# An FNet layer with a ReGLU beside it: three moved steps, and the last 192 rows of h as a twelfth pair with short products

## The chip, the cores and the metric

One core of one Trainium2 chip runs the whole program. The metric is the device time of one execution in microseconds (us); "the time before" is the median of three runs. The matmuls run on TensorE (PE in the profile), elementwise work on VectorE (DVE), ScalarE (ACT) and GpSimd (POOL). SyncE (SP) computes nothing: it issues transfers. GpSimd issues transfers too. Each engine takes its instructions from its own queue, in order.

## The reference

All data are float32, S = 2048 tokens, D = 640 features, F = 1728 hidden features of the ReGLU. Cut to what is computed:

```python
xn = (x - mean(x)) / sqrt(var(x) + 1e-5)                 # layernorm over the 640 features
a = einsum("sd,ed->se", xn, dft_hid_re)
b = einsum("sd,ed->se", xn, dft_hid_im)
fnet = einsum("ts,se->te", dft_seq_re, a) - einsum("ts,se->te", dft_seq_im, b)
gate, up = xn @ W_gate, xn @ W_up                        # 640 x 1728 each
h = gate * (gate > 0) * up                               # 2048 x 1728
out = x + fnet + h @ W_down                              # W_down is 1728 x 640
```

The three weights of the ReGLU are drawn 64 times larger than the rest. The DFT matrices are inputs like any other.

## The kernel before

**Arithmetic.** Every product is made of three matmuls (`mm3`, L127 to L132): each float32 operand is cut into a high part in TensorE's reduced format and a low part (the remainder), and the matmuls are high·high, high·low and low·high, summed in one PSUM accumulator of 128 x 512 (a bank; there are eight). `split` (L123) makes the two parts: the high by a copy on ACT (L124), the low by a subtraction on DVE (L125). Products of 2 x 2 block matrices are done by a Winograd scheme: seven products of sums and differences of blocks in place of eight, so the operands need further sums and differences on DVE.

**Phase 1, up to about 350 us: layernorm and the DFT over the sequence.** The tokens are taken in eight groups of 256 (g from 0 to 7; NH = 4 is half of them), the columns of the DFT matrices in four chunks c of 512. The host reorders the 640 features into blocks; `K14` is the first 384 of a group's columns, `K2` the last 256 (called a21 for the first four groups). For the first groups nothing can be multiplied until the layernorm has made the group's high and low, so `first_stream` (L533) interleaves group by group: for chunk 0 the products of group n (`next_products`), for chunk 1 those of the same group (`product`), and, while these run, the layernorm of group n + 1 (`next_group`, L250). The work of the engines in `next_group` is pinned in program order. It is, per group of two token rows j: statistics (L204) on DVE; the high of the next DFT block on ACT (L257); a tiny GpSimd instruction that waits for the DVE low before it (`behind_vector`, L248, writes `root_t`), and two GpSimd subtractions for the low of that DFT block (L255); square root and mean on ACT; subtraction of the mean on DVE (`ln_center`, L225), the reciprocal, the high on ACT (`ln_high`, L231), the subtraction and the high for the second j; the refined inverse root (L218 to L221); the two lows on DVE (`ln_low`, L235). For g < NH there follows the scaling of the a21 columns on DVE (L276, two instructions) and their copy to their place in SBUF, a transfer issued by GpSimd (`keep_a21`, L238 to L240). For g >= NH all 640 columns are normalised at once. In `first_stream` the split of chunk 1's DFT block (L570) is issued after the layernorm's last DVE and ACT instruction (`late["ln"]`, `late["high"]`). When the last group of the first half is through chunk 0, `keep_first` (L593) copies the three accumulators of chunk 0 out on ACT (L121), since the second half uses the same banks anew.

**Phase 2, about 350 to 745 us: gate, up and h.** 26 blocks `gate_up(n)`, 13 of 128 hidden features for each half q of the tokens, plus `gate_up_rest` for the last 64 features. The blocks of h go to memory: `hd[q]` holds 13 blocks of 128 rows, `hrest[q]` the last 64. Beside the blocks DVE and ACT prepare what phase 3 needs of W_down and of the DFT over the hidden axis: `pair_weights(k, n)` (L966) loads pair k of two 128-row blocks of weights in block n - 1, makes four sums on DVE and a high and a low in block n, and stores them (1 MB) to `wparts` from GpSimd's queue in block n + 1. There are NPAIR = 11 pairs, five of the DFT and six of W_down, at blocks 13 to 23. At the very end `lead_load` and `lead_split` (L1003, L1009) prepare the first unit of phase 3.

**Phase 3, from 730 us to the end: `project(q)` for q = 1, then 0.** Out of the results of phase 1 (`pqd`) and h, out = x + fnet + h @ W_down is formed in transposed tiles of 128 features x 512 tokens: five feature blocks, two column chunks per half. The contraction consists of six units of one or two pairs each: three of the DFT over the hidden axis (pairs (0, 1), (2, 3), (4)) and three of h (pairs (0, 1), (2, 3), (4, 5)), that is rows 0 to 1535 of h. Seven Winograd products run over the units one after another: B11, T1, B21, T2, B22, T3, T4. A unit has three steps: `load` (transfers issued by SP), `prepare` (for T1, T2, T3, T4 a subtraction of two raw tiles on DVE, L1110; the split into the ring buffer; the split of the weights where they come raw) and `run` (the matmuls on two accumulators, on three for B11, T1, B21 and B22). `read` adds finished accumulators to tiles y on DVE (`add_y`, L1214), which `get_y` (L1206) has filled with x from memory (L1211); `get_y` stands behind each product's fourth unit.

Rows 1536 to 1663 of h (the thirteenth block) and the last 64 rows are not in a pair: `plain_block` and `plain_rest` prepare them beside product B21, and `plain_run` multiplies them plainly, with three matmuls per tile for the block and two for the 64 rows (high and low of these are stacked on the 128 partitions). In each half these are ten tiles of five matmuls: three tiles behind B21, three behind B22, and behind T3 the two tiles `("o", i)`, which hold the plain product alone, and the two accumulators ("a", i) that T4 then adds to.

**What sets the order.** `drive(far, ahead)` (L722) walks through the list `todo`: at position i it issues the prepare step of position i - 2, the load of position i, the reading of i - 5 and the matmuls of i - 4. In phase 3 the engines SP and GpSimd keep this written order (`manual_schedule`, L1266); a scheduler orders PE, DVE and ACT around the pins, where `in_turn` (L138) holds a split behind the third last low. In phase 2 PE, DVE and ACT are in written order. The tile pools of phase 3 (L1056) are rings: `ring2` has 3 buffers, `wts` 5, `wraw` 4, `raws` 24; a transfer into a buffer waits until its former content has been used, and a pool that lies over the memory of phase 2 waits for the last use there. The y tiles of before lie over a weight buffer of phase 2 (`gw1`), whose last use is the lead unit's.

Of the kernel before, what the change touches and what calls it, by code (L numbers as in the profile page):

```python
# [7 lines left out]
F32 = mybir.dt.float32  # L8
# [43 lines left out]
NPAIR = KD + NF // 2  # L52
# [6 lines left out]
def fnet_reglu_kernel(  # L59
# [190 lines left out]
    def next_group(g, b, raw, before):  # L250
# [18 lines left out]
        late["high"] = pin([ln_high(g, xs, mv, 1, cs)])[0].ins  # L269
# [4 lines left out]
        late["ln"] = pin(ln_low(g, xs, j, cs) for j in range(SG))[-1].ins  # L274
        if g < NH:
            late["ln"] = pin(nc.vector.tensor_scalar(xs[:, j, K2], xs[:, j, K2], mv[:, j, 0:1], stat[:, 1, g, j : j + 1],  # L276
                                                     op0=OP.subtract, op1=OP.mult) for j in range(SG))[-1].ins
# [255 lines left out]
    def first_stream(c, name, g):  # L533
# [25 lines left out]
        def prepare():  # L559
# [4 lines left out]
            if (n > 0 or c > 1) and "b" not in t:  # L564
# [401 lines left out]
    def pair_weights(k, n):  # L966
# [3 lines left out]
        def load():  # L970
            t["z"] = z = pool("prep").tile([P, Y12 + 2 * P], F32, name="pw")
            wa, wb = pair(k, 1)
            for w, o1, o2 in ((wa[0], Y11, Y21), (wb[0], Y12, LOW + Y22)):
                nc.sync.dma_start(z[:, o1 : o1 + 2 * P], w[:, : 2 * P])
                nc.sync.dma_start(z[:, o2 : o2 + 2 * P], w[:, 3 * P :])
# [16 lines left out]
    def pair(k0, n):  # L992
# [3 lines left out]
        f = 2 * (k0 - KD)  # L996
        w = wd[f * P : (f + 2 * n) * P].rearrange("(k i p) n -> k i p n", i=2, p=P)
# [58 lines left out]
    for n, b, side in (("wraw", 4, "left"), ("ring2", 3, "left"), ("wts", 5, "left"), ("raws", 24, "left"), ("plain", 1, "right"), ("y", 1, "right")):  # L1056
        open_pools[n] = ctx.enter_context(tc.tile_pool(name=n, bufs=b, side=side, reuse_waits="tile"))

    def project(q):
        c0, c1 = 2 * q, 2 * q + 1  # L1060
        units = [("hid", u) for u in HID_UNITS] + [("f", u) for u in F_UNITS]
        raws, B, y, plain = {}, {}, {}, {}

        def get(kind, u):
            what, ks = units[u]
            o = raws[kind, u] = pool("raws").tile([P, 2, CH], F32, name="rw")[:, : len(ks)]
            col, row = int(kind in ("B12", "B22")), int(kind in ("B21", "B22"))
            if what == "hid":
                nc.sync.dma_start(o, pqd[(c0, c1)[col]][row][:, ks[0] : ks[-1] + 1])
            else:  # L1070
                nc.sync.dma_start(o, hd[q][2 * ks[0] + row : 2 * ks[-1] + row + 1 : 2, :, col * CH : (col + 1) * CH].rearrange("f p t -> p f t"))  # L1071

        def unit(name, u, first):
            what, ks = units[u]
            n, k0 = len(ks), ks[0] + (KD if what == "f" else 0)
# [3 lines left out]
            def load():  # L1079
# [6 lines left out]
                ahead = {("B21", 1): 0, ("B21", 3): 1, ("B21", 5): 2, ("T2", 0): 3, ("T2", 2): 4, ("T2", 3): 5}.get((name, u))  # L1086
# [4 lines left out]
                own, sums = [i.rearrange("k p n -> p k n") for i in pair(k0, n)], wparts[:, k0 : k0 + n]  # L1091
                if name in PARTS:
# [13 lines left out]
            def prepare():  # L1106
# [5 lines left out]
                with in_turn():  # L1112
# [9 lines left out]
                    elif name == "T4":  # L1122

                        src = r("B21")
                        sub(src, src, r("B12"))
# [3 lines left out]
                    lows.append(split(b[:, 0], b[:, 1], src))  # L1129
                    if "r" in t:  # L1130
# [3 lines left out]
            def run():  # L1134
# [5 lines left out]
                for out, oo, more in [((key, i), o + i * P, more) for i in range(2)] + ([(row4[1], row4[0], name in ("B21", "B22"))] if row4 else []):  # L1140
                    if first and not more:
                        B[out] = bank()
                    for j in range(n):
                        mm3(B[out], (w[:, j, 0, oo : oo + P], w[:, j, 1, oo : oo + P]), (b[:, 0, j], b[:, 1, j]),
                            first and not more and j == 0, u == len(units) - 1 and j == n - 1, more)

            return load, prepare, run

        def plain_block():


            def load():
                plain["r"] = r = pool("plain").tile([P, W2 + D], F32, name="pr")
                nc.sync.dma_start(r[:, :W2], hd[q][NF - 1])
                if q == 1:
# [151 lines left out]
```

## Time and profile before

| | |
|---|---|
| time, median of 3 runs | 1030.93 us (1029.65, 1030.93, 1031.65) |
| the profiled execution | 1030.23 us, of which the span 1028.3 us |
| granted TensorE clock, mean | 1.000 |
| PE busy | 1022.1 us, 4528 matmuls |
| DVE busy | 805.9 us (78%) |
| ACT busy | 427.6 us (42%) |
| POOL busy | 118.1 us (11%) |
| DMA | 242.73 MB, mean 236 GB/s |

A row of the timeline gives the start in the span, a duration (of a run of instructions where "x4" stands at its end: from the start of the first to the end of the last), the engine and line, the operation, what it writes and reads (program names, without buffer numbers), tile shapes, and in brackets the time the engine had been idle before and who ended it. A matmul's duration overlaps the next one's; its cost is the distance between two starts. "SPq" and "POOLq" are rows of queues: an instruction there that issues a transfer and may wait first.

### The profile page before, as it was taken

Reading aid. Unit: us, or ns where it says so; the run is one execution under the profiler, and the core shown is the slowest. Engines: PE = TensorE matmul, PEld = TensorE weight load, DVE = VectorE, ACT = ScalarE, POOL = GpSimd, SP = SyncE. Lnnn points to the kernel's source line nnn. Section 1 sums busy time; section 2 is a strip of 40 time slices with the busy share of each in tenths; the row PEclk is TensorE's granted clock in tenths of the full one; section 3 lists DMA queues with packets and bytes.
Section 4 is the critical chain, followed back from the end, with each engine's and each line's share of the span. In section 5 each row is a group of like instructions: output and inputs, shape, how many; then the busy total and the mean of one; then the engine's idle time right before and its main releaser. Section 6 shows DMA issues by size and latency. Waiting matters only on the chain.

```text
span 1028.3 us, 12486 instructions
## 1 busy us (share of the span) xinstructions
PE 1022.1 (99%) x4528; PEld 844.5 (82%) x4528; DVE 805.9 (78%) x1089; ACT 427.6 (42%) x534; POOL 118.1 (11%) x184
## 2 busy tenths in 40 slices
PE   9999999999999999999999999999999999999998
PEld 7888888888888888888888888888888888888886
DVE  8967987998989586788878988886597666886764
ACT  5554453343433333433335443443355423552531
POOL 3431001012110002411110001000000000000000
PEclk9999999999999999999999999999999999999999
DMA  7987734968969785763474665662699647986543
GB/s 304 342 278 274 265 124 164 338 221 262 349 229 348 299 323 165 249 213 136 153 237 152 225 228 216 230 255 103 237 346 302 189 132 232 357 322 213 156 154 122
DMA packets 101469, 242.73 MB, mean 236 GB/s; under 512 B 11552, under 2 KB 50976, under 8 KB 98848
## 3 DMA queue, kind: packets, MB, share of 16 engines
q1 hardware_dynamic: 83664, 171.68, 48.6%
q0 software_dynamic: 17744, 70.26, 18.6%
q8 instruction: 35, 0.57, 0.2%
q14 instruction: 26, 0.21, 0.1%
HBM read 182.12 MB, written 58.74 MB: 234 GB/s over the span
## 4 chain that ended last, share of the span: by engine, by line
PE 98%; DMA 1%; DVE 0%; SPq 0%; ACT 0%; issue 0%; DVEq 0%
PE ps L132 31%; PE ps L131 31%; PE ps L130 31%; PE ps L481 3%; PE ps L1204 1%; PE ps L510 1%; DMA rw<-hd 1%; DMA r<-in_x 0%; SPq L1211 0%; DVE wt L125 0%; DVE bs L204 0%; DVE y L1214 0%; ACT cb L292 0%; SPq L1100 0%; SPq L1071 0%
## 5 line engine op out<-in xcount | busy, mean ns | idle before, releaser
L132 PE MATMUL ps<-cb,wt 128*128 128x512 f32 x390 | 151.9, 390 | 0.4 <-DVE wt L125 0.4
L130 PE MATMUL ps<-cb,wt 128*128 128x512 f32 x390 | 151.8, 389 | 0.0
L131 PE MATMUL ps<-cb,wt 128*128 128x512 f32 x390 | 151.7, 389 | 0.0
L125 DVE TENSOR_TENSOR cb<-rw,cb 128x1024 fp32r<-128x1024 f32 x83 | 94.0, 1132 | 68.4 <-ACT cb L124 66.9
L124 ACT ACTIVATE cb<-rw 128x1024 fp32r<-128x1024 f32 x83 | 82.0, 988 | 147.3 <-PE ps L132 127.6
L124 ACT ACTIVATE cb<-raw 128x1024 fp32r<-128x1024 f32 x71 | 75.3, 1060 | 114.2 <-PE ps L132 107.8
L125 DVE TENSOR_TENSOR cb<-raw,cb 128x1024 fp32r<-128x1024 f32 x71 | 86.8, 1222 | 40.3 <-ACT cb L124 40.1
L132 PE MATMUL ps<-xs_early,gw 128*128 128x512 f32 x260 | 101.2, 389 | 0.0
L131 PE MATMUL ps<-xs_early,gw 128*128 128x512 f32 x260 | 101.2, 389 | 0.0
L130 PE MATMUL ps<-xs_early,gw 128*128 128x512 f32 x260 | 101.1, 389 | 0.0
L130 PE MATMUL ps<-cb,xs_late 128*128 128x512 f32 x232 | 90.2, 389 | 0.0
L131 PE MATMUL ps<-cb,xs_late 128*128 128x512 f32 x232 | 90.2, 389 | 0.0
L132 PE MATMUL ps<-cb,xs_late 128*128 128x512 f32 x232 | 90.2, 389 | 0.0
L121 ACT ACTIVATE gw<-z 128x1024 fp32r<-128x1024 f32 (+1 forms) x52 | 57.6, 1109 | 76.4 <-DVE z L814 76.4
L131 PE MATMUL ps<-cb,xs_early 128*128 128x512 f32 x226 | 88.0, 390 | 0.0
L132 PE MATMUL ps<-cb,xs_early 128*128 128x512 f32 x226 | 87.9, 389 | 0.0
L130 PE MATMUL ps<-cb,xs_early 128*128 128x512 f32 x226 | 87.9, 389 | 0.0
L132 PEld LDWEIGHTS ps<-cb,wt 128*128 128x128 f32 x390 | 73.2, 188 | 16.0 <-DVE wt L125 0.7
L131 PEld LDWEIGHTS ps<-cb,wt 128*128 128x128 f32 x390 | 73.2, 188 | 15.4
L130 PEld LDWEIGHTS ps<-cb,wt 128*128 128x128 f32 x390 | 73.2, 188 | 15.2
L121 ACT ACTIVATE u<-ps 128x512 f32<-128x512 f32 x52 | 31.1, 597 | 94.0 <-PE ps L132 94.0
L824 DVE TENSOR_TENSOR gw<-z,gw 128x1024 fp32r<-128x1024 f32 (+1 forms) x52 | 64.6, 1283 | 3.8 <-ACT gw L121 3.8
(190 smaller groups left out, 1983.1 us busy)
## 6 DMA issues: line engine op xcount, KB each, us to landing
raw<-in_dft SPq DMA_DIRECT2D x94, 512.0 KB, 5.5
wt<-wparts SPq DMA_DIRECT2D x66, 256.0 KB, 3.2
z<-in_wgu SPq DMA_DIRECT2D x26, 640.0 KB, 4.0
hd<-ob POOLq DMA_DIRECT2D x26, 512.0 KB, 3.7
rw<-hd SPq DMA_DIRECT2D x24, 512.0 KB, 6.4
wparts<-pw POOLq DMA_DIRECT2D x11, 1024.0 KB, 4.1
tk<-in_dft SPq DMA_DIRECT2D x16, 512.0 KB, 6.1
set<-r POOLq DMA_DIRECT2D x16, 512.0 KB, 4.0
```

Source lines behind the costliest of these rows:

```text
L121: return nc.scalar.activation(o, i, AF.Copy)
L124: nc.scalar.activation(hi, src, AF.Copy)
L125: return nc.vector.tensor_tensor(lo, src, hi.bitcast(F32), op=OP.subtract)
L130: nc.tensor.matmul(ps, wh, mh, start=first, stop=False, skip_group_check=more)
L131: nc.tensor.matmul(ps, wh, ml, start=False, stop=False, skip_group_check=more)
L132: nc.tensor.matmul(ps, wl, mh, start=False, stop=last, skip_group_check=more)
L481: start["pe"] = pin([nc.tensor.matmul(E[0, key], xn_part(n * SG + j, d)[v == 1], b[:, int(v == 2), j], start=False, stop=n % NH == NH - 1 ...
L510: pin([nc.tensor.matmul(E[c, key], xn_part(j, d)[v == 1], b[c][0][:, int(v == 2), j], start=j == 0 and v == 0, stop=False)])
L824: tt(self.w[:, 1, cs], self.z[:, cs], self.w[:, 0, cs].bitcast(F32), op=OP.subtract)
L1204: nc.tensor.matmul(B[key], wr[:, v, es], hr[:, cs], start=False, stop=v == 1, skip_group_check=not new)
```

## The change

Three moves, and a twelfth pair:

- The scaling of a21 and its copy leave `next_group` and become `scale_a21()`, called behind the split of chunk 1's DFT block (L570 of before) in `first_stream`.
- In group g = NH the second j's high (ACT) and low (DVE) are deferred into `late["second"]`, which `keep_first` calls behind its three copies.
- In the product B11 of q = 1, `get_y` stands behind the last unit and not behind the fourth.
- NPAIR becomes 12: rows 1536 to 1663 of h with the last 64 rows as pair 11, whose second block has 64 rows and is filled up with zeros in the weights (in block 24 of phase 2) and in the raw tile of B22. `project` has a seventh unit `("end", (6,))`. In the products B21, B22 and T4 this unit's contraction has only 64 rows that are not zero: its operands are stacked, high over low, on 128 partitions, and two matmuls do what three did (`short`). `plain_block`, `plain_rest`, `plain_run`, the tiles `("o", i)` and the pool `plain` go; a pool `ends` of four one-block tiles comes in. `get("B22", 6)` stands in T2's fifth unit. In T4 the last two units change places, so that the end unit is not the last. T3's reading of ("a", i) now finishes the tile.

```diff
-NPAIR = KD + NF // 2
+NPAIR = KD + NF // 2 + 1
...
-        late["high"] = pin([ln_high(g, xs, mv, 1, cs)])[0].ins
+        if g != NH:
+            late["high"] = pin([ln_high(g, xs, mv, 1, cs)])[0].ins
...
-        late["ln"] = pin(ln_low(g, xs, j, cs) for j in range(SG))[-1].ins
+        late["ln"] = pin(ln_low(g, xs, j, cs) for j in range(SG)[: 1 if g == NH else SG])[-1].ins
+        if g == NH:
+            def second():
+                late["high"] = pin([ln_high(g, xs, mv, 1, cs)])[0].ins
+                late["ln"] = pin([ln_low(g, xs, 1, cs)])[0].ins
+            late["second"] = second
         if g < NH:
-            late["ln"] = pin(nc.vector.tensor_scalar(...) for j in range(SG))[-1].ins
-            keep_a21(g)
+            late["a21"] = g, xs, mv
...
+    def scale_a21():
+        if "a21" not in late:
+            return
+        g, xs, mv = late.pop("a21")
+        late["ln"] = pin(nc.vector.tensor_scalar(xs[:, j, K2], xs[:, j, K2], mv[:, j, 0:1], stat[:, 1, g, j : j + 1],
+                                                 op0=OP.subtract, op1=OP.mult) for j in range(SG))[-1].ins
+        keep_a21(g)
...
                 if c == 1 and n < NG - 1:
                     late["ln"] = i.ins
+                    scale_a21()
...
                 pin([copy(t["first"][:, i], E[c, key])])
+            late["second"]()
...
+            if wb.shape[0] < P:
+                for o in (Y12, LOW + Y22):
+                    nc.gpsimd.memset(z[REST:, o : o + 2 * P], 0.0)
...
+        if f == NF - 1:
+            return wd[None, f * P : NF * P], wd[None, NF * P :]
...
-    for n, b, side in (... ("plain", 1, "right"), ("y", 1, "right")):
+    for n, b, side in (... ("ends", 4, "right"), ("y", 1, "right")):
...
+        units = [...] + [("end", (NF // 2,))]
...
+            elif what == "end" and row:
+                if col:
+                    nc.gpsimd.memset(o[b2], 0.0)
+                nc.sync.dma_start(o[a, 0], hrest[q][:, col * CH : (col + 1) * CH])
...
+            short = what == "end" and name in ("B21", "B22", "T4")
...
+                if short and name == "T4":
+                    t["w"] = w = weights()
+                    for rows, v, o in ((a, 0, HIGH), (b2, 0, LOW), (a, 1, LOW), (b2, 1, HIGH)):
+                        nc.sync.dma_start(w[rows, 0, v, : 2 * P].bitcast(F32), sums[a, 0, o + Y22 : o + Y22 + 2 * P])
+                    return
...
+                    if short:
+                        lows.append(split(b[a, 0], b[b2, 0], src[a]))
...
+                    if "r" in t and short:
+                        t["w"] = w = weights()
+                        r = t["r"][a]
+                        split(w[a, :, 0], w[a, :, 1], r)
+                        copy(w[b2, :, 1], r)
+                        sub(w[b2, :, 0], r, w[a, :, 0].bitcast(F32))
...
+                    if short:
+                        for v in range(2):
+                            nc.tensor.matmul(B[out], w[:, 0, v, oo : oo + P], b[:, 0, 0], start=False, stop=last and v == 1, skip_group_check=more)
+                        continue
...
-        def plain_block():
...
-        def plain_rest():
...
-        def plain_run(tiles):
...
-                return [(2 + i, 1, ("a", i), False) for i in two]
-            if name == "own":
-                return [(2 + i, 1, ("o", i), "late") for i in two]
+                return [(2 + i, 1, ("a", i), True) for i in two]
...
-            for u in range(len(units)):
-                l, p, r = unit(name, u, u == 0)
+            us = list(range(len(units)))
+            if name == "T4":
+                us[-2:] = us[:-3:-1]
+            for u in us:
+                end = u == us[-1]
+                l, p, r = unit(name, u, u == 0, end)
...
-                if u == 3:
+                if u == (len(units) - 1 if (name, q) == ("B11", 1) else 3):
                     todo.append(((lambda name: lambda: get_y(name))(name), idle, idle, idle))
...
-            if tiles:
-                todo.append((idle, idle, (lambda t: lambda: plain_run(t))(tiles), ...))
-            if name == "T3":
-                todo.append((idle, idle, lambda: plain_run([(("a", i), 2 + i, 0) for i in range(2)]), idle))
```

More of the change, by code (lines that the diff above doesn't have):

```diff
@@ L1122, in prepare @@
                     elif name == "T4":
[L1124 to L1125 removed]
+                        src, at = r("B21"), a if short else slice(0, P)
+                        sub(src[at], src[at], r("B12")[at])
                     else:
@@ L1195, in plain_run @@
-        def plain_run(tiles):
-            for key, e, c in tiles:
-                new = key not in B
-                if new:
-                    B[key] = bank()
-                cs, es = slice(c * CH, (c + 1) * CH), slice(PLACE[e] * P, (PLACE[e] + 1) * P)
-                (w, wr), (h, hr) = (PW["w"], PW["wr"]), (plain["h"], plain["hr"])
-                mm3(B[key], (w[:, 0, es], w[:, 1, es]), (h[:, 0, cs], h[:, 1, cs]), new, False, not new)
-                for v in range(2):
-                    nc.tensor.matmul(B[key], wr[:, v, es], hr[:, cs], start=False, stop=v == 1, skip_group_check=not new)
```

86 lines of the change are left out of this document (27 added, 59 removed).

## The prediction

> **What bounds the kernel now.** I read the busy shares of the engines first, then the shares of the chain that ended last, then that chain's longest pieces in order of time (start, duration, engine, line, count), and last TensorE's own timeline at the places where its matmuls were not at their usual distance.
>
> ```profile
> PE 1022.1 (99%) x4528; PEld 844.5 (82%) x4528; DVE 805.9 (78%) x1089; ACT 427.6 (42%) x534; POOL 118.1 (11%) x184
> PE 98%; DMA 1%; DVE 0%; SPq 0%; ACT 0%; issue 0%; DVEq 0%
> 64.29 4.08 PE ps L481 x18
> ```
>
> TensorE is 98% of the chain. Undisturbed, 18 matmuls take 4.08 us: 0.2267 us from one start to the next, whatever the product. So the time is the number of matmuls, plus the few places where TensorE stands still. These are the starts at three of them (start, duration, line, count):
>
> ```profile
> 18.71 0.39 PE L130 MATMUL ps<-cb,xs_early 128*128 128x512 f32 x1
> 19.06 0.50 PE L131 MATMUL ps<-cb,xs_early 128*128 128x512 f32 x1
> 19.40 0.40 PE L132 MATMUL ps<-cb,xs_early 128*128 128x512 f32 x1
> ...
> 39.37 1.35 PE L481 MATMUL ps<-cb,xs_late 128*128 128x512 f32 x4
> ...
> 745.34 0.39 PE L131 MATMUL ps<-cb,wt 128*128 128x512 f32 x1
> 746.08 0.50 PE L132 MATMUL ps<-cb,wt 128*128 128x512 f32 x1 [0.35 <-DVE wt L125]
> 746.42 0.40 PE L130 MATMUL ps<-cb,wt 128*128 128x512 f32 x1
> ```
>
> At 18.71 two distances of 0.35 and 0.34 lose 0.24 us. At 39.37 four matmuls take 1.35 where 3 x 0.227 + 0.39 = 1.07 would do: 0.28. At 745.34 the distances 0.74 and 0.34 lose 0.63. The distance after a stop is 0.34 each time, so a stop costs its length and 0.11. All three moves aim at these 1.15 us.
>
> **The twelfth pair: matmuls.** Before, the last 128 rows of h and the 64 after them are multiplied plainly. L1204 is the part for the 64 rows, two matmuls a tile:
>
> ```profile
> L1204 PE MATMUL ps<-hr,wq 128*128 128x512 f32 x40 | 12.4, 392 | 0.0
> ```
>
> So there are 20 tiles, 10 per half q, and `plain_run` adds three matmuls a tile for the 128 rows: 5 x 20 = 100. As a pair they are seven products with 18 outputs per half: B11, T1, T2, T3 with 3 + 3 + 2 + 2 = 10 outputs of 3 matmuls, and the short B21, B22, T4 with 3 + 3 + 2 = 8 outputs of 2. That is 46 per half, 92 in all. 8 x 0.2267 = **1.81 us gained**.
>
> **The twelfth pair: what lies beside.** Its weights (four sums, a high, a low) are made in gate/up block 24. There DVE has 2.5 us more, ACT 0.85, POOL two clears and a store, SP four loads:
>
> ```profile
> 692.00:702.00 10.00, 2.47 (x5) 0.85 (x1) 0.53 (x1) 1.00 0.38 157
> 710.00:720.00 10.00, 10.00 (x46) 8.29 (x45) 3.90 (x5) 2.39 (x4) 0.53 (x1) 1.00 0.13 52
> 880.00:920.00 40.00, 40.00 (x178) 33.14 (x177) 32.62 (x36) 22.41 (x26) 1.08 (x2) 1.00 0.92 324
> ```
>
> The first row is the busy time of the instructions on the eleventh pair's weights (DVE, ACT, POOL), the second all work of the core just behind the place of the new ones (PE, weight loads, DVE, ACT, POOL, then clock, DMA share, GB/s). DVE is free for 6.1 of these 10 us, and the accumulators that it then reads up to 2.5 us later are wanted again only two blocks (some 24 us) on: I take nothing; without that cover it would be up to 2.5. Project's loads change too: by the shapes 2.1 MB per half in place of 1.7 and 1.0. The fullest stretch for them is the first two products of the second half, the third row, with DMA at 0.92 and 324 GB/s. There the pair adds 0.9 MB and 18 matmuls, 4.1 us: 220 GB/s, less than what already flows, so nothing again; if the loads were the bound there it would be 0.9 MB / 324 GB/s = 2.8 us less the 4.1, still no loss. Its splits on ACT and DVE stand between those of the other units.
>
> **Where a cover goes: T3 to T4.** The plain tiles stood between T3 and T4: 20 matmuls, 4.5 us, in which DVE read T3's two accumulators. Now T4's first matmul adds to the first of them at once. How soon can it be read? (The first two rows are the last matmul of a unit of T4 and the split of a later unit that needs its ring buffer, the next two the last matmul on an accumulator and its reading.)
>
> ```profile
> 1011.40 0.39 PE L132 MATMUL ps<-cb,wt 128*128 128x512 f32 x1
> 1012.97 1.23 DVE L125 TENSOR_TENSOR cb<-rw,cb 128x1024 fp32r<-128x1024 f32 x1 [3.55 <-ACT cb L124]
> ...
> 1022.28 0.39 PE L132 MATMUL ps<-cb,wt 128*128 128x512 f32 x1
> 1022.71 0.69 DVE L1214 TENSOR_TENSOR y<-ps,y 128x512 f32<-128x512 f32 x1 [4.43 <-PE ps L132]
> ...
> 851.10 1.22 DVE L1110 TENSOR_TENSOR rw<-rw 128x1024 f32<-128x1024 f32 x1
> 852.24 1.22 DVE L125 TENSOR_TENSOR cb<-rw,cb 128x1024 fp32r<-128x1024 f32 x1
> 857.90 1.28 DVE L1214 TENSOR_TENSOR y<-ps,y 128x512 f32<-128x512 f32 x2
> ```
>
> A read starts 0.43 after its accumulator's last matmul and takes 0.69; with 0.04 to TensorE the bank is free 1.16 us after that matmul. T3's last unit is one pair: behind the first accumulator's last matmul come three for the second, so T4's first is due 4 x 0.227 = 0.91 after it. 0.25 + 0.11 is the least. DVE's queue decides what is added. In the changed order it holds, ahead of that read, the split of T4's first unit and one subtraction (1.14 each, from start to start). The split starts 1.57 after the last matmul that used its buffer, as in the first two rows; that matmul is 19 matmuls (4.31 us) ahead of T4's first, so split and subtraction end at -4.31 + 1.57 + 2.28 = -0.46, and the accumulator is ready at -0.91 + 0.43 = -0.48. DVE is 0.02 late: 0.38 per half, **0.76 lost**. The second accumulator is read behind two more splits and is due eleven matmuls later; with 0.3 to spare that holds. Bounds: 0 if the read is early, 1.5 per half if one full operation (1.22) comes in front.
>
> **The third move: loads of y behind the first product's other loads.** SP's queue, and a piece of the chain:
>
> ```profile
> 735.10 1.29 SPq L1211 DMA_DIRECT2D y<-in_xt  x3
> ...
> 737.49 7.55 DMA rw<-hd
> ```
>
> The three loads wait until 735.1 for memory of the phase before, and the loads of the fifth and sixth units wait behind them. Moved behind, the fifth unit's go at about 727, the sixth's behind a weight buffer at 734.5; y lands long before its reading at about 755. I take the whole **0.63 as gained**; 0 if memory holds those loads too.
>
> **The first two moves.** At 18.71 the matmul waits for a low that DVE makes after scaling a21 (L276). Moved behind the low, the scaling (0.65) lets it finish at 18.4: 0.24 gained there. At 39.37 the matmuls wait for three copies of accumulators (ACT L121), which stand behind both highs of the normalisation (L231, 1.55 for the two). One of them, 0.74 of it, goes behind the copies: 0.28 gained. But the scaling's end also starts POOL's copy of a21 (L240), and POOL's two lows for the next group (L255) stand behind that copy in its queue. DVE, POOL and ACT rows (a count of 2 or 3 joins neighbours):
>
> ```profile
> 17.14 0.73 DVE L276 TENSOR_SCALAR r<-r,mv,stat 128x256 f32<-128x256 f32 x2
> 17.79 1.22 DVE L125 TENSOR_TENSOR cb<-raw,cb 128x1024 fp32r<-128x1024 f32 x1
> 20.96 1.06 DVE L225 TENSOR_SCALAR r<-r,mv 128x384 f32<-128x384 f32 x1
> 22.01 0.40 DVE L225 TENSOR_SCALAR r<-r,mv 128x384 f32<-128x384 f32 x1
> 28.28 1.11 DVE L225 TENSOR_SCALAR r<-r,mv 128x384 f32<-128x384 f32 x1
> 44.09 0.50 DVE L225 TENSOR_SCALAR r<-r,mv 128x640 f32<-128x640 f32 x1
> 44.63 1.47 DVE L225 TENSOR_SCALAR r<-r,mv 128x640 f32<-128x640 f32 x1
> ...
> 18.20 0.88 POOL L240 DMA_DIRECT2D xs_early<-r  x1 [4.72 <-DVE r L276]
> 19.25 2.54 POOL L255 TENSOR_TENSOR cb<-raw,cb 128x512 fp32r<-128x512 f32 x2
> 42.88 2.86 POOL L255 TENSOR_TENSOR cb<-raw,cb 128x512 fp32r<-128x512 f32 x2 [0.40 <-ACT cb L257]
> ...
> 29.50 1.13 ACT L231 ACTIVATE xs_early<-r,mv 128x384 fp32r<-128x384 f32 x2 [0.71 <-DVE mv L210]
> 36.79 1.55 ACT L231 ACTIVATE xs_late<-r,mv 128x640 fp32r<-128x640 f32 x2 [0.83 <-DVE mv L210]
> 38.37 1.57 ACT L121 ACTIVATE sa<-ps 128x512 f32<-128x512 f32 x3
> ```
>
> The subtraction of the mean (L225) takes 0.40 alone, and 1.06 or 1.11 when POOL is in a low: it ends 0.22 after POOL (19.25 + 2.54, against 22.02). Before, its first half meets POOL's second low and its second half is free. Now the scaling ends at 19.0 instead of 17.87, so POOL's lows run from 20.4 instead of 19.25. The first half, still due at 20.96, waits out the first low and ends at 21.9; then POOL's second low goes, and the second half waits for that too. This pattern is in the trace at 44.09: 0.50, then 1.47. It ends at 23.2, not 22.41.
>
> From there by the same distances: these 0.8 us, and 0.5 more for the scaling that now lies behind the low (0.65, less what DVE waited for ACT), put the next group's subtraction at 29.6 instead of 28.28. POOL's lows, 0.3 + 0.75 behind the scaling's end at 27.65, run from 28.85 to 31.5 and meet it again. Its first half ends at 30.35, ACT's high (0.62) at 31.1; TensorE wants it at 30.93 and loses 0.2 + 0.11. One group on DVE is 1.9 late; ACT's first high ends at 39.3 and the three copies stand behind it, to 40.8. TensorE wants the third bank at 39.86: 0.97 + 0.11. So 1.40 us of stops in place of 0.24 + 0.28: the two moves **lose 0.88**. Bounds: -0.52 if nothing meets, +2.35 if POOL's second low goes first each time (first halves end near 23.1, 31.9, 39.9). I take the middle, since at 44.09 DVE went first.
>
> The Trainium skill weighs on this: its page "SBUF — State Buffer", section "Who interferes with whom", says that a DVE instruction in a two-port mode and a GpSimd instruction exclude each other for the whole instruction, and whoever issues first has the ports. The trace agrees (1.06 against 0.40). By that rule the waiting first half goes before POOL's second low and the sum stays -0.80; costed without it, the moves pay 0.52 and the sum is -2.20.
>
> **Sum.** -1.81 + 0.76 - 0.63 + 0.88 = -0.80 us. The profiled execution took 1030.23 (span 1028.3 and 1.93 around it), so 1029.43; the median, 1030.93, is 0.70 above it: **1030.1 us**. 0.2% is 2.06 us, about what a measurement of this kernel can tell from no change.
>
> **Rivals.**
> - The start moves pay as they read, since POOL's lows miss DVE's subtractions: -1.81 + 0.76 - 0.63 - 0.52 = -2.20, 1028.7. For it: two stops are visible and their causes are moved. Against: POOL's queue order. With T4's wait hidden as well: 1028.0.
> - POOL's second low takes its turn first: +0.67, 1031.6. For: it directly follows the first. Against: the row at 44.09.
> - The third move cures nothing, other memory waits hold the fifth unit's loads: -0.17, 1030.8. Against: neighbouring loads of the same kind go before the wait.
> - Slower: DVE becomes the bound before T4. From T3's start to the first read it does ten operations of 1.14 and six of 0.60, 15.0 us, in 15.8; before, 20 plain matmuls gave it 4.5 more. Each us beyond the 0.8 of slack is paid in both halves; from 2.2 us of lag (1.43 more per half) the kernel is 2.06 slower, 1033.0. For: DVE's rows stand without gaps around 851 to 859. Against: nothing there lasts longer than its kind elsewhere.
>
> **How the numbers follow.** Forecast 0.43 (its own range 1029.3 to 1031.0), moves pay 0.28, POOL first 0.11, third move idle 0.07, DVE bound 0.11. Faster by over 0.2%, below 1028.9: two thirds of the second with tails: 0.24. Slower: the last and a tail: 0.13. Same: 0.63. The range reaches from the second case with T4's wait hidden, 1028.0, to the third plus 0.4 (half the spread between the runs is 1.0): 1028.0 to 1032.0; it leaves out the last and the fastest end.
>
> **What would show it.** TensorE with 4520 matmuls. POOL's L255 from about 20.4, and L225 pairs near 20.96 and 29.6 both long; TensorE stops near 31 and of about 1 us near 40. No stop near 745. A stop of about 0.4 at T4's first matmul in both halves, released by DVE's reading of y. I am wrong if TensorE passes 31 and 40 unbroken, or stops by over 1 us at T4.

## The result: 1035.9 us, slower by 0.57%

The changed kernel takes 1035.9 us in the median of six runs (1034.82 to 1039.99), the kernel before 1031.27 in the runs beside it. The ratio is 1.0057, with a 95% interval of 1.0047 to 1.0068. Two of the six runs, 1038.55 and 1039.99 us, weigh in the ratio but not in the medians, which lie 4.63 us (0.45%) apart. The prediction had 1030.1, and 1028.0 to 1032.0 as its range.

The first lines of the page of the changed kernel, engines and the shares of the chain that ended last:

```profile
PE 1023.6 (99%) x4520; PEld 843.0 (82%) x4520; DVE 821.4 (79%) x1117; ACT 433.5 (42%) x552; POOL 121.3 (12%) x191
PE 92%; DMA 3%; DVE 3%; ACT 1%; SPq 0%; issue 0%; ACTq 0%; DVEq 0%
```

The eight matmuls are gone (4520 for 4528), but TensorE is 92% of the chain and not 98%: transfers, DVE and ACT have come in. The last matmul starts at 1029.59 us in the span, and started at 1023.64 before: 5.95 us. TensorE's timeline at the start, with the matmul ahead of each of the first two stops:

```profile
22.76 0.39 PE L132 MATMUL ps<-cb,xs_early 128*128 128x512 f32 x1
24.13 1.20 PE L496 MATMUL ps<-cb,xs_early 128*128 128x512 f32 x4 [0.98 <-ACT xs_early L231]
32.21 0.39 PE L132 MATMUL ps<-cb,xs_early 128*128 128x512 f32 x1
32.97 0.73 PE L496 MATMUL ps<-cb,xs_early 128*128 128x512 f32 x2 [0.37 <-ACT xs_early L231]
42.15 1.72 PE L496 MATMUL ps<-cb,xs_late 128*128 128x512 f32 x4 [0.73 <-ACT sa L121]
```

The distance from 22.76 to 24.13, in place of 0.227, loses 1.14, and 0.11 in the one behind it: 1.25 us. By the same reckoning the second stop loses 0.64 and the third 1.52; a distance of 0.34 near 15 adds 0.11. That is 3.52, where the kernel before lost 0.24 and 0.28. The same timeline in the projections:

```profile
823.38 0.50 PE L130 MATMUL ps<-cb,wt 128*128 128x512 f32 x1
824.63 0.50 PE L131 MATMUL ps<-cb,wt 128*128 128x512 f32 x1 [0.76 <-DVE cb L125]
...
864.42 0.39 PE L132 MATMUL ps<-cb,wt 128*128 128x512 f32 x1
864.97 0.47 PE L130 MATMUL ps<-cb,wt 128*128 128x512 f32 x1 [0.16 <-issue]
...
880.69 0.39 PE L132 MATMUL ps<-cb,wt 128*128 128x512 f32 x1
881.67 0.51 PE L130 MATMUL ps<-cb,wt 128*128 128x512 f32 x1 [0.59 <-ACT cb L124]
882.93 0.50 PE L131 MATMUL ps<-cb,wt 128*128 128x512 f32 x1 [0.75 <-DVE cb L125]
```

The stop at 864.97 is T4's first matmul, 0.40 us with the distance behind it; its twin in the second half, at 1013.84, is 0.41. The page names no releaser ("issue"), but DVE's rows show the reading of T3's first accumulator (L1212), which ends at 864.87:

```profile
863.05 1.22 DVE L1152 TENSOR_TENSOR rw<-rw 128x1024 f32<-128x1024 f32 x1
864.18 0.68 DVE L1212 TENSOR_TENSOR y<-ps,y 128x512 f32<-128x512 f32 x1
```

The stop at 823 to 825 (1.25) is the first unit of B22, the one at 882 (1.90) the first unit of the second half. The second half has two more, 0.72 at 966 and 0.63 at 973, around its own change from T2 to B22. There is none at 745. The whole account:

| term | predicted | measured |
|---|---|---|
| 8 matmuls fewer | -1.81 | -1.81 |
| the start (two moves) | +0.88 | 3.52 - 0.52 = +3.00 |
| the stop at 745 | -0.63 | -0.63 |
| T3 to T4, two halves | +0.76 | +0.81 |
| loads of the projections | 0 | 1.25 + 1.90 + 0.72 + 0.63 = +4.50 |
| a store of h late at 454 | 0 | +0.21 |
| sum | -0.80 | +6.08 (5.95 by the last matmul) |

What carries the two wrong terms. First the start, rows of DVE and GpSimd in the changed kernel:

```profile
21.15 2.20 DVE L225 TENSOR_SCALAR r<-r,mv 128x384 f32<-128x384 f32 x1
23.35 0.39 DVE L225 TENSOR_SCALAR r<-r,mv 128x384 f32<-128x384 f32 x1
30.19 2.00 DVE L225 TENSOR_SCALAR r<-r,mv 128x384 f32<-128x384 f32 x1
...
20.58 2.54 POOL L255 TENSOR_TENSOR cb<-raw,cb 128x512 fp32r<-128x512 f32 x2
29.43 2.54 POOL L255 TENSOR_TENSOR cb<-raw,cb 128x512 fp32r<-128x512 f32 x2
```

The first subtraction of a group begins inside GpSimd's first low and ends only when the second is over as well: 20.58 + 2.54 = 23.12, the subtraction ends at 23.35. The forecast had it end after the first low. Then the loads. SP's queue at the change of halves, in the changed kernel, then in the kernel before:

```profile
869.10 2.37 SPq L1124 DMA_DIRECT2D wt<-wparts  x4
871.57 1.05 SPq L1138 DMA_DIRECT2D wt<-wparts  x2
872.67 0.47 SPq L1093 DMA_DIRECT2D rw<-pq  x1
```

```profile
858.33 8.19 SPq L1096 DMA_DIRECT2D wt<-wparts  x4
866.57 0.47 SPq L1069 DMA_DIRECT2D rw<-pq  x1
```

The first load of the second half (rw<-pq) is issued 8.4 us ahead of T4's end (881.1) in the changed kernel, and was issued 11.1 ahead of it (877.7) before. The weight loads in front of it wait for one of five buffers, so the queue is never further than five units ahead of TensorE, and five units now hold fewer matmuls: of T4's units (12, 12, 6, 12, 12, 4, 12 matmuls) the last one's load waits for the second, 46 matmuls from the end, where before the sixth (of 12, 12, 6, 12, 12, 12) waited for the first, 54 from the end. That is 1.8 us of lead lost, and the short unit's four small loads take 2.4 us of the queue. In the same way T2's last load waits for 48 matmuls from the end instead of 54, and B22's weights stand behind it. The chain of the changed kernel shows what that costs there:

```profile
812.52 6.80 DMA wt<-wparts
819.34 2.15 DMA wr<-wparts
821.53 0.86 ACT wt L124
822.40 0.96 DVE wt L125
823.36 1.23 DVE cb L125
```

### The profile page after: what moved, and what is told of

Same layout as the page of the kernel before. It is cut to its first block, busy times and chain, and to the rows that moved or that the text cites. A ratio compares the mean times of both kernels' runs of the same rounds, so it can differ in the third digit from the quotient of the medians.

```text
span 1034.2 us, 12603 instructions
## 1 busy us (share of the span) xinstructions
PE 1023.6 (99%) x4520; PEld 843.0 (82%) x4520; DVE 821.4 (79%) x1117; ACT 433.5 (42%) x552; POOL 121.3 (12%) x191
## 4 chain that ended last, share of the span: by engine, by line
PE 92%; DMA 3%; DVE 3%; ACT 1%; SPq 0%; issue 0%; ACTq 0%; DVEq 0%
PE ps L131 30%; PE ps L132 30%; PE ps L130 30%; PE ps L496 2%; DMA wt<-wparts 1%; DMA r<-in_x 1%; DVE r L225 1%; DVE cb L125 1%; DVE bs L204 1%; PE ps L1196 1%; DMA rw<-pq 1%; DMA wr<-wparts 0%; ACT cb L124 0%; DVE r L298 0%; DVE wt L125 0%
## 5 line engine op out<-in xcount | busy, mean ns | idle before, releaser
L131 PE MATMUL ps<-cb,wt 128*128 128x512 f32 x410 | 159.9, 390 | 1.9 <-DVE cb L125 1.9
L130 PE MATMUL ps<-cb,wt 128*128 128x512 f32 x410 | 160.1, 390 | 1.4 <-ACT cb L124 0.6
L132 PE MATMUL ps<-cb,wt 128*128 128x512 f32 x410 | 159.3, 389 | 0.0
L130 PEld LDWEIGHTS ps<-cb,wt 128*128 128x128 f32 x410 | 76.9, 188 | 19.4 <-ACT cb L124 2.5
L131 PEld LDWEIGHTS ps<-cb,wt 128*128 128x128 f32 x410 | 77.0, 188 | 18.9 <-DVE cb L125 3.1
L132 PEld LDWEIGHTS ps<-cb,wt 128*128 128x128 f32 x410 | 77.0, 188 | 15.9
```

Of the source, the lines that this page charges most:

```text
L130: nc.tensor.matmul(ps, wh, mh, start=first, stop=False, skip_group_check=more)
L131: nc.tensor.matmul(ps, wh, ml, start=False, stop=False, skip_group_check=more)
L132: nc.tensor.matmul(ps, wl, mh, start=False, stop=last, skip_group_check=more)
```

## The experiments

All ratios are to the kernel before, measured in runs beside it. The whole result is computed in each of these kernels.

**The first two moves undone.** In the changed kernel:

```diff
             late["a21"] = g, xs, mv
+            scale_a21()
...
-        if g != NH:
+        if True:
             late["high"] = pin([ln_high(g, xs, mv, 1, cs)])[0].ins
...
-        late["ln"] = pin(ln_low(g, xs, j, cs) for j in range(SG)[: 1 if g == NH else SG])[-1].ins
-        if g == NH:
+        late["ln"] = pin(ln_low(g, xs, j, cs) for j in range(SG))[-1].ins
+        if False:
...
-            late["second"]()
```

> The changed kernel with the first two moves undone (scaling and copy of a21 in next_group again, second high and low of group NH in place). If the start's stops (3.52 us in the changed kernel at 15, 24, 33 and 42 us) come from the moves: the stops at 24 and 33 are gone, those of before (0.24 and 0.28) are back, and the time falls by 3.0 us. If they come from something else in the changed program (other tile places, other loads): they stay, and the time falls by less than 0.5. The stops after 800 us are the same as in the changed kernel in both.

Measured: 1031.81 us, ratio 1.0013 (1.0003 to 1.0022). No stops at 24 and 33; the two of before are back (0.23 and 0.27). The first subtraction takes what it took before:

```profile
22.48 1.07 DVE L225 TENSOR_SCALAR r<-r,mv 128x384 f32<-128x384 f32 x1
29.82 1.11 DVE L225 TENSOR_SCALAR r<-r,mv 128x384 f32<-128x384 f32 x1
```

So the moves make the start's stops. The time fell by more than the 3.0 expected: 4.5 us by the ratios (1.0057 to 1.0013), 3.4 by the medians (4.63 above the kernel before, now 1.23). In the profile the stops of the loads are 3.7 us in place of 4.5, and the store at 454 is on time, 0.2. What is left over by the ratios is not traced. The profiled execution took 1033.32 us; it has two more stops, 1.09 at 11.5 and 0.36 at 15 us. They are not of the moves: the last run below, where the scaling and the second high are moved, has the like (0.96 and 0.37).

**The copy of a21 behind GpSimd's lows.** The moves stay; `scale_a21` only notes the group, and the next `next_group` issues the copy:

```diff
             for j in range(SG):
                 low(nc.gpsimd, slice(j * CH, (j + 1) * CH))
+            if "copy" in late:
+                pin([keep_a21(late.pop("copy"))])
...
-        keep_a21(g)
+        late["copy"] = g
```

> The changed kernel, with the copy of a21 issued behind GpSimd's two lows of the next group instead of ahead of them. Theory (the copy holds GpSimd's lows until they fall on DVE's subtractions): the lows start about 1.6 us earlier, right behind the DVE low, the first L225 of a group takes 1.1 us or less instead of 2.0 to 2.3, the stops at 24 and 33 us go, and at most 0.4 us of stops is left at the start: 3 us faster than the changed kernel. Rival (the scaling itself, 0.65 us later on DVE, makes the normalisation late): L225 is short but stops of 0.5 us or more stay at 33 or 42.

Measured: 1031.84 us, ratio 1.0013 (1.0004 to 1.0023), by the medians 3.4 us faster than the changed kernel. DVE and GpSimd:

```profile
21.22 0.67 DVE L225 TENSOR_SCALAR r<-r,mv 128x384 f32<-128x384 f32 x1
21.89 0.40 DVE L225 TENSOR_SCALAR r<-r,mv 128x384 f32<-128x384 f32 x1
18.96 2.71 POOL L255 TENSOR_TENSOR cb<-raw,cb 128x512 fp32r<-128x512 f32 x2
```

No stop over 0.12 us is left between 10 and 400 us. So the scaling was moved well, and both moves together gain what they were read to gain: from the first matmul of the products to the 151st it takes 34.5 us, 35.0 before. What cost 3 us was the copy that moved with the scaling, since GpSimd's queue holds its lows behind it.

**A pause between GpSimd's two lows.** This tests the step of the prediction by which a waiting subtraction gets in between them:

```diff
             for j in range(SG):
                 low(nc.gpsimd, slice(j * CH, (j + 1) * CH))
+                if j == 0:
+                    for _ in range(2):
+                        behind_vector(before)
```

> The changed kernel with two of GpSimd's tiny instructions (root_t, about 0.15 us each from start to start) between the two lows of a group. Theory (a waiting DVE subtraction doesn't get in between two lows that follow each other at once): with the pause it does, the first L225 of a group takes 1.1 us or less instead of 2.0 to 2.3, the second one waits instead, and the start's stops fall from 3.5 us to the 1.4 that the prediction had worked out: 2 us faster than the changed kernel. Rival (GpSimd has the ports for the whole row of instructions, or it goes first whatever stands between): the first L225 still takes 2 us or more, and the time stays or grows by the 0.3 us a group.

Measured: 1032.89 us, ratio 1.0016 (1.0006 to 1.0026), by the medians 2.6 us faster than the changed kernel:

```profile
21.14 0.96 DVE L225 TENSOR_SCALAR r<-r,mv 128x384 f32<-128x384 f32 x1
22.09 0.40 DVE L225 TENSOR_SCALAR r<-r,mv 128x384 f32<-128x384 f32 x1
20.57 1.30 POOL L255 TENSOR_TENSOR cb<-raw,cb 128x512 fp32r<-128x512 f32 x1
21.82 0.72 POOL L248 TENSOR_TENSOR root_t<-cb 128x1 f32<-128x1 f32 x2
22.49 1.29 POOL L255 TENSOR_TENSOR cb<-raw,cb 128x512 fp32r<-128x512 f32 x1
```

With 0.6 us between the lows the subtraction ends 0.23 us after the first low (22.10), and even the second one fits in. The start's stops are 1.05 us, all near 40, in place of 3.52. So what the forecast missed is that DVE waits through two lows which follow each other at once.

**The moves alone,** on the kernel before, with the plain products kept.

> The kernel before with the three moves alone, the last 192 rows still multiplied plainly. Theory (the moves at the start cost 3.0 us by themselves, the later y loads gain 0.63): stops of about 1.25, 0.64 and 1.5 at 24, 33 and 42 us, none at 745, none from 800 us on; 2.4 us slower than the kernel before. Rival (the start's stops come of the changed program as a whole): the start as in the kernel before, and the time 0 to 1.2 us below it.

Measured: 1033.05 us, ratio 1.0021 (1.0012 to 1.0031): 2.2 us. The stops are 1.28, 0.64 and 1.51 us, none at 745 and none from 800 on. There is a stop of 0.28 at 454 as well. The start's loss has nothing to do with the twelfth pair.

**The second move undone** (the second high of group NH ahead of the copies again).

> The changed kernel with the second move alone undone (both highs of group NH ahead of the three copies again). If the move helps as it reads, also in the late start: the copies begin 0.84 us later, the stops at 42 to 43 us grow from 1.5 to 2.3, 0.8 us slower than the changed kernel. If the copies are held by something else: the same stops.

Measured: 1035.47 us, ratio 1.0045 (1.0029 to 1.0060), no difference from the changed kernel that the times can tell. In the profile the stop grows as expected, and brings something new (TensorE, then the busy times of 45 to 48 us: PE, weight loads, DVE, ACT, POOL, clock, DMA share, GB/s):

```profile
43.15 0.99 PE L496 MATMUL ps<-cb,xs_late 128*128 128x512 f32 x2 [1.43 <-ACT sa L121]
45.00:48.00 3.00, 3.00 (x8) 2.34 (x7) 2.91 (x6) 2.42 (x5) 1.17 (x2) 0.50 0.99 321
```

The stops up to 44 us are 2.2 us in place of 1.5, and behind them the granted clock is 0.50 for some 3 us, with 0.43 us between matmuls: some 1.6 us more. The profiled execution was the slowest of four, 1037.52 us with a mean clock of 0.998. The other three took 1034.72 to 1035.48 with 0.999 to 1.000, so the fall of the clock came in one of the four. By the profile the second move is worth its 0.7 also with a late start; the times don't show it.

**The third move undone** (y's loads behind the fourth unit again).

> The changed kernel with the third move undone (the loads of y behind the fourth unit of B11 again). If the move cured the stop at 745: it is back with 0.6 us. If the changed pools did (y lies in another place now): no stop there, and the same time as the changed kernel.

Measured: 1035.22 us, ratio 1.0053 (1.0039 to 1.0068), and no stop at 745:

```profile
744.76 0.39 PE L130 MATMUL ps<-cb,wt 128*128 128x512 f32 x1
...
745.22 0.39 PE L132 MATMUL ps<-cb,wt 128*128 128x512 f32 x1
```

SP issues y's loads at 733.83 here, and the next loads at 735.17; in the kernel before it was 735.10 and 736.44. Before, SP waited first for DVE on the weight buffer `gw` and then for TensorE; here it waits for TensorE alone. So in the changed kernel the new pools, which put y elsewhere, are enough. With the old pools the move is enough (the run above with the moves alone). Either one cures it.

**Seven weight buffers in place of five.**

```diff
-("wts", 5, "left")
+("wts", 7, "left")
```

> The changed kernel with 7 instead of 5 weight buffers in phase 3. Theory (loads are held by the ring of weight buffers, and a unit's time is shorter with the short and single units of the end pair): the weights come two units earlier, the stops at 823, 882, 966 and 973 us (1.25, 1.90, 0.72 and 0.63) go, 4.5 us faster than the changed kernel, and only the two of 0.40 at T4 stay. Rival (the DMA engines are full there, and depth doesn't help): at least half of these stops stays.

Measured: 1042.28 us, ratio 1.0115 (1.0100 to 1.0130). The stops at 823, 966 and 973 are gone; at the change of halves 2.2 us stay. The loss is elsewhere, at the change into the projections:

```profile
745.04 0.80 PE L130 MATMUL ps<-cb,wt 128*128 128x512 f32 x1 [5.57 <-ACT wt L124]
```

The larger ring moves the tiles behind it in memory, over others of the phase before: SP issues the first two loads of the projections at 727.9 and 739.5, and in the changed kernel at 720.2 and 727.3. The first units come 6 us late; the granted clock falls within the stop (0.81 from 739 to 745), is 0.50 from 745 to 748 and full again from 750. With the slower matmuls that is 8.0 us. The next run, which moves none of these tiles, has no such stop.

**An own pool for the weights of T2, T3 and T4,** with seven buffers, behind the others in memory:

```diff
-("ends", 4, "right"), ("y", 1, "right"))
+("ends", 4, "right"), ("y", 1, "right"), ("parts", 7, "right"))
...
+            parts = lambda: pool("parts").tile([P, 2, 2, 2 * P], F32R, name="wp")[:, :n]
...
                 if name in PARTS:
-                    t["w"] = w = weights()
+                    t["w"] = w = parts()
```

> The changed kernel with an own pool of 7 buffers for the weights of T2, T3 and T4, behind all other pools, so that nothing else changes its place. Theory (the ring of five weight buffers holds the queue of loads): as in the run with 7 buffers the stops at 823, 966 and 973 us (2.6 us in all) go, and without the 8 us that the moved places cost there at 745; the one at 882 stays above 1 us, since it stayed there too. 2.6 us faster than the changed kernel. Rival (what went away there went because TensorE was 8 us late and the loads were not): they stay.

Measured: 1035.44 us, ratio 1.0043 (1.0028 to 1.0058). The stops at 823, 966 and 973 are gone, so the ring held these loads. At the change of halves 1.7 us stay. The time did not follow: 1.4 us less by the ratios (1.0057 to 1.0043), which their intervals don't tell from none, and nothing by the medians (4.60 above the kernel before, for 4.63). The profile's stops behind 800 us are 2.8 less; the reason was seen only in a later run.

**The first load of the second half issued early,** behind the load of T4's fifth unit:

```diff
     for q in (1, 0):
         project(q)
+        if q:
+            second = len(todo)
+    early = todo[second][0]
+    todo[second] = (idle, *todo[second][1:])
+    load = todo[second - 3][0]
+    todo[second - 3] = (lambda: (load(), early()), *todo[second - 3][1:])
```

> The changed kernel with the load of the second half's first unit (B11, DFT pairs 0 and 1) issued right behind the load of T4's fifth unit, ahead of the two last loads of T4. Theory (its transfers are issued too late, behind weight loads that wait for a buffer): they start near 866 us instead of 872.7, and the stop of 1.9 us at 882 goes, the others stay; 1.9 us faster than the changed kernel. Rival (the DMA engines are full there, so another load becomes late in its place): a stop of 1 us or more stays within the next 10 us.

Measured: 1034.4 us, ratio 1.0039 (1.0024 to 1.0054). SP's queue, and ACT's wait for the weights:

```profile
868.36 0.55 SPq L1093 DMA_DIRECT2D rw<-pq  x1
868.96 0.86 SPq L1142 DMA_DIRECT2D wr<-in_hid  x1
878.36 0.85 ACT L124 ACTIVATE wt<-wr 128x768 fp32r<-128x768 f32 x1 [3.60 <-DMA wr<-in_hid]
```

Issued 11 us before T4 ends (880.4), the load of the weights is used when it lands, 9.4 us on; in the changed kernel its like took at most 6.7 (873.18 to 879.83). The stop is 1.1 us in place of 1.9, as the rival has it. Both theories have a part: the issue was late, and the earlier transfer took longer, at a DMA share of 0.96 from 868 to 879. The time says little on this: the profile has other stops than the changed kernel's, 1.4 us between 818 and 827 and 1.8 at 456.

**The last two units of T3 in reversed order** (`if name in ("T3", "T4")`).

> The changed kernel with the last two units of T3 in reversed order, as T4 has them, so that six matmuls and not three lie behind the first accumulator's last one. Theory (T4's first matmul waits for the reading of that accumulator): the stops of 0.40 us at 865 and 1014 go, 0.8 us faster. Rival (DVE's queue is late by its splits, or T4's weights are): they stay or grow.

Measured: 1037.27 us, ratio 1.0063 (1.0046 to 1.0079). The stops at T4 grow to 1.5 us each. DVE's queue there:

```profile
863.38 1.22 DVE L1152 TENSOR_TENSOR rw<-rw 128x1024 f32<-128x1024 f32 x1
864.51 1.22 DVE L125 TENSOR_TENSOR cb<-rw,cb 128x1024 fp32r<-128x1024 f32 x1
865.65 0.68 DVE L1212 TENSOR_TENSOR y<-ps,y 128x512 f32<-128x512 f32 x1
```

The accumulator is complete earlier, but the reading (L1212) has a subtraction and a split in front of it in the new order and comes at 865.65; TensorE goes on at 866.43. The expectation fell, the prediction's reckoning stands: the place in DVE's queue sets this stop.

**Late copy, own pool and early load together.**

> The changed kernel with three edits together: the copy of a21 behind GpSimd's lows, the own pool of 7 for the weights of T2, T3 and T4, and the early load of the second half's first unit. By the runs so far: matmuls -1.81, the start -0.5 and the transition -0.63 against the kernel before, the two stops at T4 +0.8, and at the change of halves 0 (if the load is early enough now that no weight load ahead of it waits) to 1.7 us: 0.4 to 2.1 us faster than the kernel before, 1028.6 to 1030.4. Rival (the loads only push each other, and a stop of 1 us or more comes up at another product): not faster than the kernel before.

Measured: 1031.09 us, ratio 1.0007 (0.9998 to 1.0015). After 10 us only 1.7 us of stops are left, 0.76 up to 870.0 (DVE's low is late), 0.38 at each T4 and 0.18 at 732. That should have been enough. The missing time is in the matmuls themselves (33 distances lie between the two rows of each pair). Here, and then in the changed kernel:

```profile
805.88 0.39 PE L132 MATMUL ps<-cb,wp 128*128 128x512 f32 x1
813.58 0.40 PE L132 MATMUL ps<-cb,wp 128*128 128x512 f32 x1
```

```profile
807.35 0.39 PE L132 MATMUL ps<-cb,wt 128*128 128x512 f32 x1
814.83 0.39 PE L132 MATMUL ps<-cb,wt 128*128 128x512 f32 x1
```

7.70 / 33 = 0.2333 us a matmul against 7.48 / 33 = 0.2267. The 428 matmuls of T2, T3 and T4 lose 2.8 us by it. The clock is full. The buffers of the new pool start 32 bytes ahead of a multiple of 512 in the partition's bytes; those of the ring of before start on such multiples.

**The same with 992 bytes more beside the pool:**

```diff
-("parts", 7, "right")
+("pad", 1, "right"), ("parts", 7, "right")
...
+    open_pools["pad"].tile([P, 992 // 4], F32, name="pad")
```

> The run with the late copy, the own pool of weights and the early load again, with 992 bytes more beside the pool, so that its buffers start at a multiple of 512 bytes of their partition and not 32 bytes ahead of one. In the runs with that pool each matmul whose weights lay there took 0.2333 us instead of 0.2267, 404 pairs of them within one accumulator. Theory (the weights' address does it): 0.2267 again, and the time falls by 2.6 us, to 1027.9 to 1028.5, 0.2% faster than the kernel before. Rival (the region of memory, or the row stride of 256 instead of 384 numbers): still 0.2333 and the same time.

Measured: 1028.53 us (1027.56 to 1029.71), ratio 0.9975 (0.9966 to 0.9984): 0.25% faster than the kernel before, and 0.8% faster than the changed one. The matmuls:

```profile
806.17 0.39 PE L132 MATMUL ps<-cb,wp 128*128 128x512 f32 x1
813.65 0.39 PE L132 MATMUL ps<-cb,wp 128*128 128x512 f32 x1
```

7.48 / 33 again. The address was it: the pool lies 992 bytes away from its first place, and the row stride is the same in both runs. Only these two places were tried. At the change of halves no stop is left. This is the version to keep.

## Why the prediction was wrong

**The bound, and the matmuls saved:** right. 8 x 0.2267 us went.

**T3 to T4:** right in size, 0.40 and 0.41 for 0.38 a half, and right in its reckoning: the reading starts at 864.18, 0.45 after its accumulator's last matmul (863.74) and just as DVE's subtraction before it ends. In the reversed order of T3 DVE's queue alone sets it. That the size fits to 0.02 is partly luck: from the end of the reading to TensorE it took 0.10, where the prediction had 0.04 (in the kernel before it is 0.06 at 746.08), and the distance behind the stop was 0.31 and not 0.34.

**The stop at 745:** right in size. That the move does it was only half the truth: the changed pools alone do it too. The rival "third move idle" expected the stop to stay, and fell with it; so did "DVE becomes the bound before T4", since these stops stayed at 0.40.

**"I take the middle, since at 44.09 DVE went first":** wrong; +3.00 for +0.88. The row at 44.09 showed a subtraction that started just as the first low ended (42.88 + 1.3), not one that had been waiting; there GpSimd's second low waited instead, and the two took 2.86 in place of 2.54. Where one waits, it waits through both lows: 2.20, 2.00 and 2.29 us. The order of causes was right: the copy holds the lows, the lows hold DVE, and TensorE stops at 24, 33 and 42 (31 and 40 were named, the first was not). On the way, 0.3 + 0.75 behind 27.65 is 28.70 and not 28.85; the lows began at 29.43. The rival "POOL's second low takes its turn first" is what happened, and its price, 2.35 for the start, was 0.65 too small. The Trainium skill's rule ("SBUF — State Buffer", "Who interferes with whom": whoever issues first has the ports for the whole instruction) was read so that a waiting DVE instruction would go ahead of GpSimd's next one. These runs show that it doesn't when the next one follows at once, and that it does with 0.6 us between.

**"So nothing again", on the loads of the projections:** wrong, and the largest error: +4.50. The argument was on bandwidth, over a stretch of 40 us: the pair's bytes over its matmuls are less than what already flows. But the loads are issued in order, at most five weight buffers ahead, and what counts is the time from an issue to the use of its data. Single and short units are units like the others for the ring, and hold 6 or 4 matmuls in place of 12. So lead went from 12.2 to 10.9 us (T2) and 10.4 us (T4), by my own count of matmuls, while the loads took 6 to 9 us to land and ACT and DVE need 2 to 3 more. The plain tiles, which the prediction looked at only as DVE's cover, were also matmuls without loads: time for the queue to get ahead. The row 880:920 was called the fullest stretch (740 to 780 is fuller, 0.95 and 337 GB/s), but the stops at 823, 966 and 973 came in stretches that had been far from full before (DMA share 0.53 from 800 to 830, then 0.76).

**Not foreseen:** 0.21 us at 454, where ACT's copy into a buffer of h waits for the store of its former content, which lands 9.7 us after its issue (8.7 in the kernel before, where TensorE loses nothing). The loss was between 0 and 1.8 us in these kernels' profiles, 0.28 with the moves alone; what sets it was not tested.

**What stays open:** how the loss at the change of halves divides between late issue and full transfer engines (1.1 of 1.9 us stayed with the early load alone, 1.7 with the own pool alone, nothing with both), the 0.77 at 869 in the last run, and why the clock fell in one execution of a kernel and not in the others.

## What to carry to other kernels

When a unit of work is made shorter, ask every ring that counts in units how much time its depth is now worth; a product without loads that is taken away is also a rest for the queue of loads. When an instruction is moved, follow what it releases on the other queues: here a copy that waited for it stood ahead of work that keeps a third engine waiting. And when a run that should be faster isn't, compare the distance of undisturbed instructions, not only the stops.

## What the runs showed of the hardware

- A DVE subtraction that waits while GpSimd is in an elementwise instruction also waits through the next one if that follows at once: 2.20 and 2.00 us for 128 x 384 (0.40 alone), 2.29 for 128 x 640 (0.53 alone). With 0.6 us of tiny GpSimd instructions in between (0.9 the third time) the three took 0.96, 0.77 and 1.05.
- Matmuls of 128 x 512 took 0.2333 us from start to start with weights in buffers that begin 32 bytes ahead of a multiple of 512 bytes, and 0.2267 with 992 bytes more in front of them and nothing else changed.
- In one profile, after stops of 1.6, 0.26 and 0.26 us within 3 us, the granted clock fell to 0.50 for about 3 us; three other executions of that kernel have a mean clock of 0.999 to 1.000 and took 2 us less, so the stops of one program don't bring it every time. In another, in a stop of 5.6 us, it fell before the stop's end and was full again within 5 us after it. The changed kernel, with 0.9, 0.26 and 0.26 at the first place, kept the full clock in its profile. The Trainium skill's page "TensorE: Matmul & The Clock Gate" ("Part 1: The HAM clock gate") has the clock halved after an idle window of about 3.4 us. The second case agrees; in the first the longest idle time was 1.43 us, and the clock fell all the same.
